# Band attention and a bilinear unit on one core: global queries over six spans of three key chunks instead of eight spans of two, with a new order of all steps

## The chip, the cores and the metric

One core of a Trainium2 chip runs the whole kernel. The metric is the device time of one execution in microseconds; the time before is the median of three runs.

## What is computed

For 8 batches and 8 heads of 64 columns there are 512 local tokens, each of which attends to the local tokens at most 32 away and to 32 global tokens, and the 32 global tokens, which attend to all 544 keys. The result goes through a bilinear unit and two products.

```python
s_g = scale * np.matmul(q_g, k_all.transpose(0, 1, 3, 2))   # k_all: 32 global and 512 local keys
out_g = np.matmul(sm(s_g), v_all)
mask = np.abs(pos[:, None] - pos[None, :]) <= 32
s_l = np.concatenate([scale * q_l @ k_g.T, np.where(mask, scale * q_l @ k_l.T, -1e9)], axis=-1)
out_l = np.matmul(sm(s_l), v_all)
x = np.concatenate([out_g, out_l], axis=2)                  # as 8 * 544 rows of 512
out = ((x @ w1) * (x @ w2) @ w3) @ w_out
```

## The kernel before

**Units.** Attention works on pairs of heads, m = 0 to 31 (four pairs for each batch). For a pair the keys lie in an SBUF tile K with the head's 64 columns on the partitions, as 16 local chunks of 32 keys and one global chunk; a spread copy (`spread_k`, L321) puts chunk n + 1 and the global chunk side by side, so that `window(m, h, n)` (L327) reads four blocks of 32 keys at once: chunk n - 1, chunk n, chunk n + 1 and the global keys. The tile V holds the same four blocks on its four strips of 32 partitions.

**Local queries.** `scores` (L335) takes 32 products of 64x32 weights with 128 columns into one PSUM tile, VectorE takes a masked minimum of the negated scores (L356), ScalarE exponentiates (L361), VectorE transposes 32x32 blocks (L369), four DMAs write to DRAM and one reads it back with the blocks on their strips (L375, L380); `values` (L393) multiplies with V.

**Global queries.** A unit u is two pairs, that is four heads; there are 16 units. `g_scores` (L460) uses the window at the eight odd n = 1, 3, ... 15 of each pair. Only chunk n - 1 and n count there; the next chunk is masked as it comes again, and the global keys count at n = 9 alone. That is 2 pairs x 8 spans x 2 heads = 32 products. `g_minus_max` (L473) runs once for each head, `g_max` (L480) combines the minima of four partition strips in six small VectorE instructions, `g_exps` (L489) runs once for each head, the 128x1024 tile G is transposed (L369) and goes through DRAM (L375, L380), and `g_values` (L495) has eight products for each of four heads and four products of one column that sum the exponentials (L508). `g_normalize`, `g_back`, `g_copy` and `g_out` (L511 to L527) finish the unit.

**Weights and the unit after attention.** Weights arrive packed as 64-bit words and are unpacked by ScalarE and VectorE (`unpack`, L605). w3 and w_out are first multiplied with each other (`fold`, L695, 64 products of 512 columns in fp32, L698). Then `first` (L542), the gate on ScalarE and VectorE (`gate_a` to `gate_lo`, L555 to L569) and `second` (L571) run over 17 tiles of 256 tokens in four quarters each, 68 gates, with split high and low parts. A gate is: copy of one factor, multiply (L561), cast, subtraction.

**What sets the order.** Every step has a number in a table written out by hand (`ORDER_OF`, L40), and its letter picks the engine where there is a choice (A is ScalarE, D VectorE, P GpSimd). `in_order` (L190) sorts by these numbers, and each engine runs its steps in that order. All DMAs are issued from SyncE's queue. An issue in that queue waits for the DMA eight issues before it to land, besides what its buffer waits for. At the start, `warm` (L869) runs ten products of zeros on TensorE, and `constants`, `clear` and `edges` (L247 to L272) set up masks and the identity.

Of the kernel before, what the change touches and what calls it, by code (L numbers as in the profile page):

```python
# [11 lines left out]
ALU = mybir.AluOpType  # L12
# [6 lines left out]
def i(ap):  # L19
# [8 lines left out]
PAD = (48, 0)  # L28

# [11 lines left out]
    load="3 11 7 56 1 20 31 124 139 107 170 191 150 226 260 233 393 287 234 312 317 421 357 445 432 551 450 679 597  "  # L41
# [5 lines left out]
    clear="4 5 117",  # L47
    edges="12",
    warm="9",
    fetch="0 14 2 15 19 26 41 45 60 71 68 72 79 95 120 115 123 131 132 152 165 177 190 178 250 251 261 259 301 360 349  "  # L50
    "380 283 350 412 409 460 491 498 471 502 542 554 520 581 595 602 555",
    unit="16 10 17 22 21 30 28 6 35 37 29 42 33 25 50 40 32 52 58 43 59 57 51 61 65 70 85 87 89 102 86 80 98 101 92  "
# [7 lines left out]
    fold="34 64 74 94 119 138 147 160 48 93 97 109 161 166 185 208 47 67 73 113 125 127 146 149 62 66 91 122 126 137  "  # L60
    "151 159 216 218 223 231 236 242 248 253 252 254 263 290 307 309 314 316 305 318 328 330 394 425 429 436 335  "
    "363 381 382 395 402 404 410",
    w34h="A179 A217 D158 A164 A284 A322 A437 D423",
    w34l="184 219 168 171 299 329 439 431",
    vc="A23 P83 A8 A39 P298 A46 P278 P368 A516 P479 A546 A398 P559 A575 A673 D663 A801 D711 A800 D807 A881 P768  "
# [3 lines left out]
    vs="A96 P105 A84 D163 A141 A227 P194 P156 A288 P213 P271 P201 A343 A355 A240 P274",  # L69
    kc="P13 D18 A54 P53 A136 A116 P202 P200 P270 P277 P339 A336 A483 A505 A529 A530 D658 D665 P725 A695 P799 A795  "  # L70
# [3 lines left out]
    s="24 77 189 238 324 367 514 582 676 730 815 858 924 981 1058 1135 1206 1265 1334 1405 1470 1540 1621 1672  "  # L74
    "1748 1815 1892 1943 2027 2079 2164 2219",
    mm="38 44 75 55 49 36 27 63 153 103 134 104 130 155 90 135 198 196 192 210 220 197 214 195 279 246 303 280 267  "
# [10 lines left out]
    ex="99 81 76 118 88 69 78 82 167 180 176 121 203 157 129 143 239 257 206 235 241 209 258 215 297 344 345 321  "  # L87
# [11 lines left out]
    tp="181 186 207 230 264 291 353 364",  # L99
    pt="D182 A187 A228 A256 A289 D304 A383 A391",  # L100
    v="193 262 325 403 524 590 684 746 816 888 923 1038 1078 1165 1216 1276 1381 1437 1510 1547 1645 1730 1750  "
    "1839 1904 1972 2026 2121 2168 2277 2333 2355",
    iv="175 222 323 362 495 552 669 701 778 847 916 957 1048 1123 1188 1253 1292 1398 1468 1530 1604 1666 1740 1798  "
    "1868 1929 2020 2070 2150 2204 2329 2348",
    nm="199 300 346 415 549 640 693 760 840 898 944 1047 1101 1173 1244 1288 1389 1456 1527 1556 1654 1735 1791  "
    "1858 1916 1991 2049 2126 2192 2295 2337 2370",
    xt="225 310 358 424",
    xh="A232 A255 A319 D333 A369 D371 A428 A444 P686 D709 P723 A733 P796 D826 A808 D828 D970 P1012 D978 P1017 D1077  "
    "P1098 P1086 A1111 P1260 A1201 P1294 A1287 D1339 P1399 P1351 D1400 A1513 A1493 D1587 D1562 A1602 A1651 P1643  "
    "D1722 A1779 A1805 A1873 P1852 P1886 D1988 D1909 P2006 D2061 P2035 A2122 D2125 A2167 A2196 P2179 D2230 A2343  "  # L110
    "P2345 P2363 D2390 D2397 D2504 P2431 A2510",
    xl="269 266 334 340 387 414 438 585 D702 D759 P724 D734 D813 D874 D812 P873 D985 P1043 D1001 D1021 D1087 D1157  "
# [91 lines left out]
def band_attention_glu_kernel(  # L204
# [62 lines left out]
    def edges():  # L267
# [3 lines left out]
        for x in range(0, 128, 32):  # L271
            nc.gpsimd.tensor_copy(pick[x : x + 32], ident[x : x + 32, x : x + 32])  # L272
# [797 lines left out]
```

## Time and profile before

| | |
|---|---|
| median of three runs | 768.01 us (766.51 to 769.08) |
| profiled execution, its own time | 763.19 us |
| its span on the core | 761.4 us |
| mean granted TensorE clock | 0.991 |
| busy: TensorE, VectorE, ScalarE, GpSimd | 98%, 60%, 38%, 14% of the span |
| DMA queue of SyncE | 136.61 MB, 63.3% of 16 engines |

Engines are named as the profile does: PE is TensorE (PEld its weight loads), DVE VectorE, ACT ScalarE, POOL GpSimd, SP SyncE (SPq its queue of DMA issues). A PE group's "mean ns" is the length of one record, and records overlap, so busy time divided by the count is the pace. An fp32 product appears as two records. The granted clock is a share of 2.4 GHz.

### The profile page before, as it was taken

Reading aid. Unit: us, or ns where it says so; the run is one execution under the profiler, and the core shown is the slowest. Engines: PE = TensorE matmul, PEld = TensorE weight load, DVE = VectorE, ACT = ScalarE, POOL = GpSimd, SP = SyncE. Lnnn points to the kernel's source line nnn. Section 1 sums busy time; section 2 is a strip of 40 time slices with the busy share of each in tenths; the row PEclk is TensorE's granted clock in tenths of the full one; section 3 lists DMA queues with packets and bytes.
Section 4 is the critical chain, followed back from the end, with each engine's and each line's share of the span. In section 5 each row is a group of like instructions: output and inputs, shape, how many; then the busy total and the mean of one; then the engine's idle time right before and its main releaser. Section 6 shows DMA issues by size and latency. Waiting matters only on the chain.

```text
span 761.4 us, 25319 instructions
## 1 busy us (share of the span) xinstructions
PE 748.4 (98%) x10564; PEld 654.5 (86%) x10564; DVE 454.0 (60%) x1385; ACT 292.1 (38%) x904; POOL 108.0 (14%) x162
## 2 busy tenths in 40 slices
PE   5999999999999999999999999999999999999998
PEld 3455689899998999998989999999999999999997
DVE  3689787766664656565667466755566566333322
ACT  4788875544232433224515243432335311210000
POOL 2126541010301100011002011011001120100000
PEclk7999999999999999999999999999999999999999
DMA  8998987888568477565788666775675787310000
GB/s 280 305 297 261 219 244 209 237 225 234 143 179 228 125 217 197 170 167 140 205 248 221 183 169 185 203 204 148 183 226 125 202 227 209 101 58 28 1 28 28
DMA packets 97850, 138.22 MB, mean 182 GB/s; under 512 B 15656, under 2 KB 58280, under 8 KB 97736
## 3 DMA queue, kind: packets, MB, share of 16 engines
q1 hardware_dynamic: 97736, 136.61, 63.3%
q8 instruction: 83, 1.36, 0.7%
q14 instruction: 31, 0.25, 0.1%
HBM read 96.71 MB, written 39.85 MB: 179 GB/s over the span
## 4 chain that ended last, share of the span: by engine, by line
PE 95%; DVE 1%; DMA 1%; POOL 0%; SPq 0%; issue 0%; ACT 0%; DVEq 0%; POOLq 0%
PE ap L551 9%; PE acc L581 9%; PE bp L551 8%; PE bp L552 8%; PE acc L583 8%; PE bp L553 8%; PE acc L582 8%; PE ap L552 8%; PE ap L553 8%; PE w L698 8%; PE s L349 5%; PE v L399 4%; PE sg L469 2%; PE gx L505 2%; DMA q<-in_q_t_dram 1%; DMA cs<-in_cst_dram 1%
## 5 line engine op out<-in xcount | busy, mean ns | idle before, releaser
L551 PE MATMUL ap<-x,w12h 128*128 128x256 f32 x512 | 145.0, 283 | 0.0
L551 PE MATMUL bp<-x,w12h 128*128 128x256 f32 x512 | 144.1, 281 | 0.0
L552 PE MATMUL ap<-x,w12h 128*128 128x256 f32 x512 | 142.1, 278 | 0.0
L552 PE MATMUL bp<-x,w12h 128*128 128x256 f32 x512 | 142.1, 278 | 0.0
L553 PE MATMUL ap<-x,w12l 128*128 128x256 f32 x512 | 142.0, 277 | 0.0
L553 PE MATMUL bp<-x,w12l 128*128 128x256 f32 x512 | 141.9, 277 | 0.0
L361 ACT ACTIVATE P<-P,mn 128x128 f32<-128x128 f32 x256 | 100.7, 396 | 63.5 <-issue 34.3
L551 PEld LDWEIGHTS ap<-x,w12h 128*128 128x128 f32 x512 | 96.2, 188 | 3.9 <-issue 2.0
L551 PEld LDWEIGHTS bp<-x,w12h 128*128 128x128 f32 x512 | 96.2, 188 | 3.8 <-issue 1.4
L552 PEld LDWEIGHTS bp<-x,w12h 128*128 128x128 f32 x512 | 96.4, 188 | 1.9
L552 PEld LDWEIGHTS ap<-x,w12h 128*128 128x128 f32 x512 | 96.3, 188 | 1.1
L553 PEld LDWEIGHTS ap<-x,w12l 128*128 128x128 f32 x512 | 96.3, 188 | 0.0
L553 PEld LDWEIGHTS bp<-x,w12l 128*128 128x128 f32 x512 | 96.3, 188 | 0.0
L356 DVE CUSTOM_DVE_ANT_0 P<-s,cs 128x128 f32<-128x128 f32 x256 | 62.8, 281 | 34.4 <-PE s L349 31.4
L698 PE MATMUL w<-wo,w3f 128*128 128x512 f32 x128 | 61.7, 627 | 2.1 <-DVE wo L612 1.5
L315 POOL COPY V<-vg 32x1024 f32<-32x1024 f32 x29 | 30.8, 1067 | 137.3 <-PE gx L508 96.0
L698 PEld LDWEIGHTS w<-wo,w3f 128*128 128x128 f32 x128 | 24.2, 199 | 29.4 <-issue 23.1
L361 ACT ACTIVATION_READ_ACCUMULATOR P<-P,mn 128x1 f32 x256 | 48.5, 190 | 0.0
L493 ACT ACTIVATE G<-G,mg 128x256 f32<-128x256 f32 x64 | 32.0, 501 | 39.3 <-PE gx L508 19.6
L349 PE MATMUL s<-K,q 64*32 64x128 f32 x2048 | 37.8, 278 | 6.0 <-POOL K L325 5.8
L349 PEld LDWEIGHTS s<-K,q 64*32 64x32 f32 x2048 | 29.1, 107 | 14.8 <-issue 6.6
L369 DVE STREAM_TRANSPOSE P<-P 128x1024 f32<-128x1024 f32 x28 | 34.7, 1238 | 4.8 <-ACT P L361 4.8
(791 smaller groups left out, 1405.8 us busy)
## 6 DMA issues: line engine op xcount, KB each, us to landing
Pd<-P SPq DMA_DIRECT2D x112, 128.0 KB, 2.9
Pt<-Pd SPq DMA_DIRECT2D x28, 512.0 KB, 4.7
raw_w<-in_w_t_dram SPq DMA_DIRECT2D x24, 512.0 KB, 5.8
V<-in_v_t_dram SPq DMA_DIRECT2D x64, 192.0 KB, 4.5
K<-in_kp_t_dram SPq DMA_DIRECT2D x36, 272.0 KB, 3.8
V<-in_v_t_dram SPq DMA_DIRECT2D x36, 256.0 KB, 4.7
out_dram<-o SPq DMA_DIRECT2D x34, 256.0 KB, 3.2
q<-in_q_t_dram SPq DMA_DIRECT2D x32, 256.0 KB, 4.3
```

The costliest lines, as they stand in the source:

```text
L349: nc.tensor.matmul(block(st[:, h], x, 128 * g), q[64 * h : 64 * h + 64, c : c + 32], window(m, h, 4 * g + x), start=True, stop=True, skip_ ...
L356: nc.vector.tensor_tensor_reduce(T["P", m][:, :, h, g], chunks(T["s", m][:, h, 128 * g : 128 * g + 128]), chunks(masks[g]), -0.125, 3.0e38 ...
L361: nc.scalar.activation(P, P, AF.Exp, bias=T["mn", m][:, g, h : h + 1], scale=-1.0, accum_out=T["sm", m][:, g, h : h + 1])
L369: nc.vector.transpose(P, P)
L493: nc.scalar.activation(G, G, AF.Exp, bias=T["mg", u][:, n : n + 1], scale=-1.0, accum_out=T["lg", u][:, n : n + 1])
L551: nc.tensor.matmul(d, wh[:, k, c, :], x[:, 0, 0:w], start=(k == m % 2 == 0), stop=False, skip_group_check=True)
L552: nc.tensor.matmul(d, wh[:, k, c, :], x[:, 1, 0:w], start=False, stop=False, skip_group_check=True)
L553: nc.tensor.matmul(d, wl[:, k, c, :], x[:, 0, 0:w], start=False, stop=(k == 3), skip_group_check=True)
L581: nc.tensor.matmul(a, gh[:, m % 2, sl], wh, start=(m == 0), stop=False)
L582: nc.tensor.matmul(a, gh[:, m % 2, sl], wl, start=False, stop=False)
L583: nc.tensor.matmul(a, gl[:, m % 2, sl], wh, start=False, stop=(m == 7))
L698: nc.tensor.matmul(T["w34", t], T["w3f", t, j // 4][:, j % 4], T["wo"][:, j], start=(j == 0), stop=(j == 7))
```

## The change

The global scores use six windows around the chunks 1, 4, 7, 10, 13 and 15, and count three chunks in each (the last counts chunk 15 alone, and there the global keys). For each head the six windows fill two partition strips of three column groups, so that the four strips are two pairs by two halves: 24 score products and 24 value products for a unit instead of 32 and 32, two masked minima and two exponentials of 384 columns instead of four of 256, one combination of minima in place of two, a G of 768 columns instead of 1024, and 384 KB instead of 512 KB out to DRAM and back. The mask for it has one column for each block and is broadcast over 32 keys; the sum over strips picks the two strips of a pair. The constants' tile shrinks from 800 to 608 columns. Every number of the order is new; of that table one line stands here.

```diff
+MIDDLES = (1, 4, 7, 10, 13, 15)
...
-    sg="442 632 770 887 1018 1162 1304 1432 1573 1701 1845 1980 2114 2251 2326 2404",
+    sg="438 608 740 879 1013 1144 1274 1417 1530 1658 1797 1919 2045 2195 2271 2347",
...
-            nc.gpsimd.memset(mask_g[:, 0:128], 0.0)
-            nc.gpsimd.memset(mask_g[:, 128:256], -1.0e30)
-            nc.gpsimd.memset(mask_g[0:32, 192:224], 0.0)
+            nc.gpsimd.memset(mask_g[:, 0:9], 0.0)
+            nc.gpsimd.memset(mask_g[:, 9:12], -1.0e30)
+            nc.gpsimd.memset(mask_g[64:128, 2:9:6], -1.0e30)
+            nc.gpsimd.memset(mask_g[64:128, 11:12], 0.0)
+            nc.gpsimd.memset(pick, 0.0)
...
-        for m in (2 * u, 2 * u + 1):
-            for g in range(2):
-                for x in range(4):
-                    for h in range(2):
-                        to = st[32 * x : 32 * x + 32, h].rearrange("p (o a b g j) -> p o g a b j", o=2, a=2, b=2, g=2)
-                        nc.tensor.matmul(to[:, m % 2, g], T["qg", m // NP][64 * h : 64 * h + 64, m % NP],
-                                         window(m, h, 2 * (4 * g + x) + 1).rearrange("p a (b j) -> p a b j", b=2),
-                                         start=True, stop=True, skip_group_check=True)
+        for r in range(3):
+            for x in range(4):
+                m, c = 2 * u + x % 2, MIDDLES[3 * (x // 2) + r]
+                for h in range(2):
+                    to = st[32 * x : 32 * x + 32, h, 0:384].rearrange("p (a b r j) -> p r a b j", a=2, b=2, r=3)
+                    nc.tensor.matmul(to[:, r], T["qg", m // NP][64 * h : 64 * h + 64, m % NP],
+                                     window(m, h, c).rearrange("p a (b j) -> p a b j", b=2),
+                                     start=True, stop=True, skip_group_check=True)
...
+    def g_minus_max(u, h):
+        keep = mask_g.rearrange("p (s r) -> p s r", s=4).unsqueeze(3).to_broadcast([128, 4, 3, 32])
+        nc.vector.tensor_tensor_reduce(T["G", u][:, :, h],
+                                       T["sg", u][:, h, 0:384].rearrange("p (s r j) -> p s r j", s=4, r=3),
+                                       keep, -0.125, 3.0e38, ALU.add, ALU.min, T["mg", u][:, h : h + 1])
...
-        eng.tensor_copy(t[0:64], mg[64:128])
-        eng.tensor_tensor(mg[0:64], mg[0:64], t[0:64], ALU.min)
-        eng.tensor_copy(t[0:32], mg[32:64])
-        eng.tensor_tensor(mg[0:32], mg[0:32], t[0:32], ALU.min)
-        eng.tensor_copy(mg[32:64], mg[0:32])
+        eng.tensor_copy(t, mg[64:128])
+        eng.tensor_tensor(mg[0:64], mg[0:64], t, ALU.min)
         eng.tensor_copy(mg[64:128], mg[0:64])
...
-        for w in range(8):
-            g, x = divmod(w, 4)
+        for w, c in enumerate(MIDDLES):
+            y, r = divmod(w, 3)
             for n in range(4):
-                nc.tensor.matmul(o[32 * n : 32 * n + 32, 0:64], t[:, x, n, g], v(u, n, w),
-                                 start=(w == 0), stop=(w == 7), skip_group_check=True)
+                m, h = divmod(n, 2)
+                nc.tensor.matmul(o[32 * n : 32 * n + 32, 0:64], t[:, 2 * y + m, h, r],
+                                 Vs[(2 * u + m) % NV][:, c % 4, h, c // 4], start=(w == 0), stop=(w == 5),
+                                 skip_group_check=True)
```

**Where the order moves.** TensorE at the start of the program, before (`warm` are the products of zeros, `s` the first pair's scores, `w` the fold):

```order
L872 MATMUL warm<-og 128x128 x10
L349 MATMUL s_156<-K_75,q_131 32x128 x32
L698 MATMUL w_0_202<-wo,w3f_0_146 128x512
L698 MATMUL w_2_220<-wo,w3f_0_213 128x512
L698 MATMUL w_1_222<-wo,w3f_0_204 128x512
L698 MATMUL w_3_239<-wo,w3f_0_225 128x512
```

and after:

```order
L351 MATMUL s_153<-K_75,q_138 32x128 x32
L870 MATMUL warm<-og 128x128 x10
L698 MATMUL w_3_222<-wo,w3f_0_208 128x512
L698 MATMUL w_0_224<-wo,w3f_0_146 128x512
L698 MATMUL w_3_222<-wo,w3f_0_208 128x512
L698 MATMUL w_2_237<-wo,w3f_0_220 128x512 x2
```

The products of zeros, which stood first, now stand behind the first scores, and another fold comes first.

SyncE's queue at the same place, before (`raw_w` and `raw_wo` are packed weights, `cs` the constants, `K` and `q` those of the first pair):

```order
L662 DMA raw_w_0_99<-in_w_t_dram 128x1024
L308 DMA vg<-in_vg_t_dram 32x512
L662 DMA raw_w_0_102<-in_w_t_dram 128x1024
L248 DMA cs<-in_cst_dram 128x128
L250 DMA cs<-in_cst_dram 32x96 x4
L282 DMA K_75<-in_kp_t_dram 128x544
L279 DMA q_131<-in_q_t_dram 128x512
L662 DMA raw_wo_0_141<-in_wo_t_dram 128x1024
```

and after:

```order
L662 DMA raw_w_0_99<-in_w_t_dram 128x1024
L662 DMA raw_w_0_102<-in_w_t_dram 128x1024
L247 DMA cs<-in_cst_dram 128x128
L249 DMA cs<-in_cst_dram 32x96 x4
L662 DMA raw_wo_0_118<-in_wo_t_dram 128x1024
L284 DMA K_75<-in_kp_t_dram 128x544
L281 DMA q_138<-in_q_t_dram 128x512
L662 DMA raw_w_0_140<-in_w_t_dram 128x1024
```

The load of vg has left this place, the first `raw_wo` has moved ahead of K and q, and q stands eight places behind a weight load instead of behind vg.

GpSimd at the same place, before, with the copy that spreads the first K behind the constants:

```order
L268 COPY cs<-cs 128x2x96
L269 MEMSET cs 32x32
L270 MEMSET cs 32x32
L272 COPY cs<-cs 32x32 x4
L325 COPY K_75<-K_75 128x15x32
```

and ScalarE after, which now has that copy:

```order
L610 ACT_TABLE_LOAD
L610 ACTIVATE raw_w_0_99<-raw_w_0_99 128x512
L327 COPY K_75<-K_75 128x15x32
L610 ACTIVATE raw_wo_0_118<-raw_wo_0_118 128x512
L610 ACTIVATE raw_w_0_102<-raw_w_0_102 128x512
```

The copy of the first K has left GpSimd's queue, where it stood behind four steps that wait for the constants, for ScalarE's, where it stands behind one unpacking step.

## Rows read from the trace of the kernel before

**Rows 1.** The page, span and part 1: engine, busy us, share, instructions.
```profile
span 761.4 us, 25319 instructions
...
PE 748.4 (98%) x10564; PEld 654.5 (86%) x10564; DVE 454.0 (60%) x1385; ACT 292.1 (38%) x904; POOL 108.0 (14%) x162
```

**Rows 2.** Stretches: busy us (instructions) of each engine, granted clock, DMA share, GB/s.
```profile
core 0: us, PE busy (x) PEld busy (x) DVE busy (x) ACT busy (x) POOL busy (x), PEclk, DMA share, GB/s
40.00:50.00 10.00, 10.00 (x154) 5.57 (x152) 7.74 (x25) 7.77 (x21) 2.08 (x4) 1.00 1.04 329
300.00:400.00 100.00, 99.86 (x1631) 90.83 (x1630) 60.75 (x193) 35.28 (x122) 8.19 (x12) 1.00 0.66 184
```

**Rows 3.** TensorE's waits, longest and shortest of five: us in total, times, longest.
```profile
PE s L349 <- POOL K L325: 5.8, 1, 5.8
...
PE s L349 <- DMA q<-in_q_t_dram: 0.3, 1, 0.3
```

**Rows 4.** Groups by line, TensorE: busy us, mean ns, idle before.
```profile
L469 PE MATMUL sg<-K,qg 64*32 64x128 f32 x1024 | 18.5, 274 | 0.0
L505 PE MATMUL gx<-V,Gt 128*32 128x64 f32 x1024 | 17.7, 220 | 0.1
```

**Rows 5.** The chain of waits in order of time: start us, us, what.
```profile
87.70 2.58 PE w L698 x6
90.27 1.09 PE sg L469 x64
...
157.82 1.01 PE gx L505 x62
```

**Rows 6.** Groups by line, VectorE and ScalarE; last, the timeline of GpSimd.
```profile
L369 DVE STREAM_TRANSPOSE P<-P 128x1024 f32<-128x1024 f32 x28 | 34.7, 1238 | 4.8 <-ACT P L361 4.8
L475 DVE CUSTOM_DVE_ANT_0 G<-sg,cs 128x256 f32<-128x256 f32 x64 | 25.0, 412 | 17.3 <-PE sg L469 17.3
L415 DVE TENSOR_TENSOR vo<-v,si 128x512 f32<-128x512 f32 x32 | 21.9, 683 | 12.6 <-PE v L399 8.4 <-DMA vd<-vo 4.2
...
L493 ACT ACTIVATE G<-G,mg 128x256 f32<-128x256 f32 x64 | 32.0, 501 | 39.3 <-PE gx L508 19.6 <-PE ap L553 9.5 <-issue 6.8
...
8.26 0.34 POOL L268 COPY cs<-cs 128x192 f32<-128x192 f32 x1 [6.63 <-DMA cs<-in_cst_dram]
```

**Rows 7.** Timeline of TensorE, 0 to 20 us: start us, us, what, idle before.
```profile
1.00 4.47 PE L872 MATMUL warm<-og 128*128 128x128 f32 x20 [1.00 <-POOL og L254]
11.22 1.96 PE L349 MATMUL s<-K,q 64*32 64x128 f32 x64 [5.75 <-POOL K L325]
14.69 2.08 PE L698 MATMUL w<-wo,w3f 128*128 128x512 f32 x2 [1.51 <-DVE wo L612]
17.38 2.93 PE L698 MATMUL w<-wo,w3f 128*128 128x512 f32 x3 [0.61 <-DVE w3f L612]
```

**Rows 8.** Stretches around the turn of the clock, columns as in rows 2.
```profile
21.00:22.00 1.00, 1.00 (x3) 0.48 (x2) 0.00 (x0) 0.00 (x0) 0.00 (x0) 0.50 0.92 289
22.00:23.00 1.00, 1.00 (x4) 0.46 (x3) 0.76 (x2) 0.76 (x2) 0.00 (x0) 0.89 0.89 211
```

**Rows 9.** SyncE's queue: a wait, two issues; DMA issues, us to landing.
```profile
SPq L662 <- DMA raw_w<-in_w_t_dram: 1.5, 1, 1.5
...
1.65 0.42 SPq L662 DMA_DIRECT2D raw_w<-in_w_t_dram  x1
...
7.01 0.33 SPq L662 DMA_DIRECT2D raw_wo<-in_wo_t_dram  x1
...
raw_w<-in_w_t_dram SPq DMA_DIRECT2D x1, 512.0 KB, 5.3
...
raw_wo<-in_wo_t_dram SPq DMA_DIRECT2D x1, 512.0 KB, 4.2
...
q<-in_q_t_dram SPq DMA_DIRECT2D x1, 256.0 KB, 6.7
```

**Rows 10.** VectorE's waits at the gate's multiply: us in total, times, longest.
```profile
DVE bp L561 <- PE bp L553: 130.2, 53, 5.8
```

More of the change, by code (lines that the diff above doesn't have):

```diff
@@ L99 @@
[L99 to L105, printed above, removed]
@@ L175 @@
-    "2595 2603",
-    second="508 515 563 588 615 627 657 659 713 721 763 771 794 797 824 830 866 875 909 913 940 953 975 980 1020 1024  "
[6 rows of a table removed]
-    out="A691 A699 D852 A855 D1014 D1016 A1144 D1153 A1262 D1266 A1395 A1401 D1551 A1558 A1688 A1697 D1829 D1836  "
-    "D1967 D1971 D2109 D2116 A2228 A2233 A2346 A2364 A2460 A2462 A2526 A2528 D2569 A2571 D2609 A2610",
-    store="729 914 952 1040 1121 1061 1232 1388 1322 1505 1544 1606 1569 1614 1716 1877 1937 1907 2065 2208 2141 2306  "
-    "2256 2442 2349 2424 2505 2490 2539 2538 2590 2591 2611 2612",
+    load="3 14 7 67 47 20 30 118 116 103 175 209 162 242 333 264 350 266 275 388 282 427 428 473 456 437 502 686 581  "
[5 rows of a table added]
@@ new lines @@
+    clear="5 4 9",
+    edges="10",
+    warm="25",
+    fetch="0 6 15 16 2 28 34 45 57 35 60 64 102 89 104 113 115 161 185 164 191 192 198 247 207 251 276 283 312 286 353  "
+    "374 183 267 352 402 481 488 499 478 509 542 549 526 587 593 600 580",
+    unit="8 1 19 17 13 27 23 22 26 29 38 41 18 21 32 33 39 40 44 48 55 70 73 86 71 66 79 53 50 68 90 81 101 98 83 105  "
[7 rows of a table added]
+    fold="43 62 78 87 117 132 149 157 63 77 84 96 112 171 184 196 54 61 74 93 114 138 142 148 42 49 94 95 139 140 145  "
+    "147 213 218 223 224 229 238 262 263 237 245 271 272 274 277 287 288 294 313 319 334 358 359 364 372 369 371  "
@@ new lines @@
+    "D2317 P2325 D2370 D2443 D2369 D2434",
+    tn="461 503 622 680 747 801 876 916 1000 1058 1165 1194 1267 1336 1429 1477 1539 1596 1690 1714 1811 1865 1931  "
+    "1992 2062 2120 2224 2264",
+    po="493 540 625 689 758 804 901 966 1003 1075 1166 1199 1291 1359 1443 1483 1544 1614 1703 1764 1836 1886 1949  "
+    "2001 2084 2133 2226 2265",
+    pi="511 578 645 714 793 839 923 995 1022 1093 1189 1234 1326 1392 1451 1512 1565 1630 1727 1803 1851 1920 1963  "
+    "2046 2091 2188 2242 2278",
@@ new lines @@
+    gd="844 936 1047 1147 1329 1418 1609 1762 1869 2036 2132 2270 2339 2350 2398 2411",
+    gin="2414 2430 2436 2437",
+    gxh="P2416 A2431 D2441 A2447",
+    gxl="P2424 P2435 P2442 D2448",
+    first="449 458 440 464 485 504 505 508 533 543 548 561 606 652 616 654 660 666 675 684 701 705 709 718 722 750 756  "
[12 rows of a table added]
+    ga="A471 A512 A584 A655 A690 A708 D759 D790 D819 D862 D892 A913 D969 D993 A1017 D1071 A1108 A1123 D1139 D1169  "
[3 rows of a table added]
+    gb_="475 528 585 657 692 720 763 809 835 872 902 933 973 1024 1042 1079 1122 1142 1181 1200 1241 1285 1312 1341  "
@@ new lines @@
+    "2100 2134 2161 2183 2227 2254 2273 2310 2334 2363 2384 2400 2419 2433 2454 2466 2476 2486 2496 2509 2518  "
+    "2528 2540",
+    second="514 525 560 590 626 627 671 677 723 732 755 765 805 808 825 836 869 871 885 899 926 929 955 970 991 1007  "
[6 rows of a table added]
+    out="A695 A713 A838 D868 A984 A985 A1133 D1135 A1215 D1242 A1370 D1395 A1508 D1509 A1647 D1656 D1755 A1760 A1929  "
+    "D1942 A2069 D2071 A2169 D2198 A2286 A2289 A2397 D2404 A2458 D2462 D2504 A2507 A2543 A2546",
+    store="842 751 887 1021 1037 1154 1237 1233 1293 1364 1427 1597 1540 1664 1675 1897 1884 1786 2011 2056 2090 2233  "
@@ L187 @@
+    "2211 2296 2309 2376 2429 2415 2489 2533 2532 2531 2547 2548",
 )
@@ L233, in band_attention_glu_kernel @@
     ps_1 = ctx.enter_context(tc.tile_pool(name="ps_1", bufs=1, space=PSUM))
-    cs = const.tile([128, 800], F32, tag="cs", name="cs")
-    ident, pick = cs[:, 0:128], cs[:, 768:800]
-    mask = cs[:, 128:768].rearrange("p (n c) -> p n c", n=5)
+    cs = const.tile([128, 608], F32, tag="cs", name="cs")
+    ident, pick = cs[:, 0:128], cs[:, 528:592]
+    mask = cs[:, 128:512].rearrange("p (n c) -> p n c", n=3)
     masks = [mask[:, x] for x in (0, 1, 1, 2)]
-    mask_g = cs[:, 512:768]
+    mask_g = cs[:, 512:524]
     og = const.tile([128, 128], F32, tag="og", name="og")
@@ L372, in turned_out @@
         P = flat(T[kind, m])
-        d = T[kind + "d", m] = dram.tile([128, 4, 256], F32, tag=kind + "d", name=f"{kind}d{m}", bufs=3)
+        c = P.shape[1] // 4
+        d = T[kind + "d", m] = dram.tile([128, 4, c], F32, tag=kind + "d", name=f"{kind}d{m}", bufs=3)
         for x in range(4):
@@ L379, in turned_in @@
         t = T[kind + "t", m] = p2.tile([128, 1024], F32, tag=kind + "t", name=f"{kind}t{m}", bufs=2 if kind == "P" else 1)
-        nc.sync.dma_start(t, T.pop((kind + "d", m)).rearrange("p x c -> p (x c)"))
+        d = T.pop((kind + "d", m)).rearrange("p x c -> p (x c)")
+        nc.sync.dma_start(t[:, 0 : d.shape[1]], d)
     def transposes(m, h):
@@ L489, in g_exps @@
-    def g_exps(u, n):
-        if n == 0:
-            T["lg", u] = p2.tile([128, 4], F32, tag="lg", name=f"lg{u}", bufs=1)
-        G = T["G", u][:, :, n].rearrange("p s g j -> p s (g j)")
-        nc.scalar.activation(G, G, AF.Exp, bias=T["mg", u][:, n : n + 1], scale=-1.0, accum_out=T["lg", u][:, n : n + 1])
+        G = p2.tile([128, 1024], F32, tag="G", name=f"G{u}", bufs=NG)[:, 0:768]
+        T["G", u] = G.rearrange("p (s h r j) -> p s h r j", s=4, h=2, r=3)
+        T["mg", u] = p2.tile([128, 2], F32, tag="mg", name=f"mg{u}")
@@ L495, in g_values, with g_exps @@
+    def g_exps(u, h):
+        if h == 0:
+            T["lg", u] = p2.tile([128, 2], F32, tag="lg", name=f"lg{u}", bufs=1)
+        G = T["G", u][:, :, h].rearrange("p s r j -> p s (r j)")
+        nc.scalar.activation(G, G, AF.Exp, bias=T["mg", u][:, h : h + 1], scale=-1.0, accum_out=T["lg", u][:, h : h + 1])
     def g_values(u):
-        t = T.pop(("Gt", u)).rearrange("p (x n g q) -> p x n g q", x=4, n=4, g=2)
+        t = T.pop(("Gt", u))[:, 0:768].rearrange("p (x h r q) -> p x h r q", x=4, h=2, r=3)
@@ L507, in g_values @@
         for n in range(4):
-            nc.tensor.matmul(o[32 * n : 32 * n + 32, 64:65], pick, T["lg", u][:, n : n + 1], start=True, stop=True,
-                             skip_group_check=True)
+            m, h = divmod(n, 2)
+            nc.tensor.matmul(o[32 * n : 32 * n + 32, 64:65], pick[:, 32 * m : 32 * m + 32], T["lg", u][:, h : h + 1],
+                             start=True, stop=True, skip_group_check=True)
     def g_normalize(u):
@@ L835, in global_pair @@
         read(("sg", u), ("qg", b), ("K", m - 1), ("K", m))
-        for x in range(1, -1, -1):
-            for h in range(2):
-                add(("gm", m - x, h), "DVE", [("sg", u), ("edges",)], g_minus_max, m - x, h)
-                read(("gm", m - x, h), ("sg", u))
-        gm = [("gm", m - x, h) for x in range(2) for h in range(2)]
+        for h in range(2):
+            add(("gq", u, h), "DVE", [("sg", u), ("edges",)], g_minus_max, u, h)
+            read(("gq", u, h), ("sg", u))
         take("mt", 1, ("mt", u), ("gr", u))
-        add(("gr", u), "DVE", gm, g_max, u, nc.vector)
+        add(("gr", u), "DVE", [("gq", u, 0), ("gq", u, 1)], g_max, u, nc.vector)
         take("lg", 1, ("lg", u), ("ge", u, 0))
-        for n in range(4):
-            add(("ge", u, n), "ACT", [("gr", u), *[("ge", u, 0)] * (n > 0)], g_exps, u, n)
-            read(("ge", u, n), ("mg", u))
-        add(("gt", u), "DVE", [("ge", u, n) for n in range(4)], turn, "G", u)
+        for h in range(2):
+            add(("ge", u, h), "ACT", [("gr", u), *[("ge", u, 0)] * h], g_exps, u, h)
+            read(("ge", u, h), ("mg", u))
+        add(("gt", u), "DVE", [("ge", u, n) for n in range(2)], turn, "G", u)
         take("Gd", 3, ("Gd", u), ("go", u))
```

134 lines of the change are left out of this document (53 added, 81 removed), and 126 rows, old and new, of tables (ex, first, ga, gh).

## The prediction

> **What bounds the kernel now.** I read the page's first lines first: TensorE is busy 748.4 of 761.4 us, VectorE 454.0 [rows 1], so at most 13.0 us of the span could come from better feeding of TensorE, and the rest only from giving it less to do. Then the stretches: between 40 and 50 us its busy time is the whole stretch, between 300 and 400 us 99.86 of 100 us, while VectorE has some 40% to spare in the second [rows 2]. Then TensorE's waits: there are five in the whole run, the longest (5.8 us) for the first K window, the shortest 0.3 us for a q load [rows 3]; none is for a global step. So the path is TensorE's own queue from about 17 us to the last matmul, and anything taken out of that queue is worth its full time as long as its feeders stay early. That is the argument of this prediction.
>
> **Removed from TensorE.** Four heads' global scores take 32 matmuls now (eight spans, two pairs, two heads), 24 after; their value products 32 now, 24 after; the four sum-picking matmuls stay. An fp32 matmul of either kind shows as two records: 1024 records are 16 units of 64 [rows 4]. A scores group of 64 records lasts 1.09 us on the chain of waits, 17.0 ns per record; 62 records of a value group last 1.01 us, 16.3 ns per record [rows 5]. A new group has the same tile shapes in the same rotation over the array (four column strips, two row halves for scores; four column strips for values), so I price a removed record at the pace of the group: 16 units x 16 records x 17.0 ns = 4.35 us for scores and 16 x 16 x 16.3 ns = 4.17 us for values, together **8.5 us**. Bounds: if one record's own duration (274 ns and 220 ns [rows 4]) is a fixed part of each group, the pace is (1.09 - 0.27) / 63 = 13 ns, and 512 records give 6.7 us; by total busy time, 18.5 and 17.7 us for 1024 each [rows 4], a quarter is 9.1 us. I take 8.5, since the chain is where the time is really passed on.
>
> For the removed tiles the trace says 16 to 17 ns each. The Trainium skill ("TensorE: Matmul & The Clock Gate", Part 3, Measured speedup vs the span model) has packed tiles cost only about 4 ns each beyond the first; by that the 512 records would be worth an estimated 2 us. The trace does not agree. A rival below carries that case in the kernel's own terms.
>
> **Removed beside TensorE.** VectorE's masked minimum goes from 64 instructions of 412 ns on 256 columns to 32 on 384; even at 1.5 x 412 ns that is 19.8 us instead of 26.4. The cross-partition maximum goes from six small instructions to three per unit, the transposition covers 768 instead of 1024 columns, ScalarE's global exponentials go from 64 of 501 ns to 32 of at most 752 ns [rows 6], and each unit's trip through DRAM from 512 KB to 384 KB out and in. All of that lies under TensorE, which waits for none of it [rows 3]; I cost it at nothing. Its worth is cover: feeders get earlier. What no row shows is the masked minimum with a mask broadcast over 32 columns and one more dimension. The nearest row is the normalising multiply, which also broadcasts an operand: 683 ns for 512 columns [rows 6], no slower per column than the present minimum. Even at double price (32 x 0.8 us) VectorE would be no busier than now, so both ends are zero on the path. The changed memsets stand in GpSimd's queue ahead of the 6.63 us that it waits for the constants [rows 6].
>
> **Moved: the start.** Everything has a new place, but only before 22 us did TensorE wait for more than 0.3 us, so only there do I price the order. Now: the warming matmuls run from 1.00 for 4.47 us, then TensorE is idle until the first scores at 11.22 (1.96 us), does one fold matmul at 14.69, and from 17.38 [rows 7] runs on with no other wait than the 0.3 us [rows 3]. The granted clock is still 0.50 (the 1.2 GHz level) between 21 and 22 us and turns to 2.4 GHz early in the next microsecond [rows 8], about 22.2. So 4.8 us of folding ran at half speed and lost 2.4 us. A fold record takes 0.43 us at the full clock (2.58 us for six [rows 5]), a fold matmul 0.86. Counted as a stream at full clock that began with the first fold, it began at 17.38 + 2.4 - 0.86 = 18.9 us.
>
> After: first scores, then the warming matmuls, then folds. The first scores no longer stand behind GpSimd's constants (the K copy is on ScalarE), but their q load is one place later than a weight load, and it is the tenth DMA. Now the eleventh, the first wo load, waited 1.5 us for a raw weight load to land (the third DMA, issued at 1.65 and 5.3 us under way) and was issued at 7.01; it landed 4.2 us later, at 11.2, with twice the bytes of q [rows 9]. A DMA thus waits for the one eight places earlier. For the tenth that was vg, and is a weight load after the change, so q takes over that wait; issued near 7 and at wo's delay it lands near 11 us, at the delay of the second q load (6.7 us [rows 9]) near 13.7. I take 11.2, the time of today's first scores. Scores and warming then last 1.96 + 4.47 = 6.4 us, to 17.6, with no break on TensorE. If the clock is up by then, the stream begins at 17.6 and 1.3 us is gained; if it rises during the warming, which then gets shorter, about 2 us; if it stays low for the first folds as long as today, 2.4 us are lost again and the start is 1.1 us worse; a late q adds 2.5 us to that. Today the clock rose in unbroken work after a start with breaks; after the change the unbroken work begins some 6 us earlier, so I lean to the first case and take **1.0 us gained**, between 2 gained and 2 lost, with 3.6 lost as the far corner. The first fold's weights would have to pass VectorE by 17.6; today its counterpart came at 17.38, so this is close and is one reason why I don't take more.
>
> **Sum.** 8.5 + 1.0 = 9.5 us. The profiled execution took 763.19 us, so 753.7. That execution lies below all three runs shown (766.51 to 769.08), so I carry the ratio over: 768.01 x 753.7 / 763.19 = 758.5 us. About 0.3% (2.3 us) can be told from no change.
>
> **Rivals.**
> - *Weight supply in the fold stage.* Between 40 and 50 us the DMA engines are at a share of 1.04 with 329 GB/s [rows 2]; a 512 KB weight load is 1.6 us of that. In the new order two loads more ahead of one that a fold waits for would cost TensorE 3.2 us. Today not one fold after 17.38 waited. Together with a start that loses 1 us: 8.5 - 3.2 - 1.0 = 4.3 us, 763.7 us. Chance 0.12.
> - *The removed tiles overlapped.* If a group's length is mostly filling and switching, its 16 missing records save little: at a quarter of the shown pace 512 x 4 ns = 2 us, with the start 3.0 us, so 765.0 us. Against it: value groups of 62 and score groups of 64 records both fit one price per record, although their records last 220 and 274 ns [rows 4, 5]. Chance 0.04. The span model of the Trainium skill named above would give this.
> - *The gate becomes the wait (slower).* A second product waits for multiply, cast and subtraction of its gate, in VectorE's queue. If the new order leaves a P transposition of 1.24 us [rows 6] ahead of the multiply, TensorE stands for up to that long. There are 68 gates; the 9.5 us gained and the 2.3 us that can be told are used up from ten fully exposed gates on, and with 15 of them the time is 758.5 + 15 x 1.24 = 777 us. Against it: VectorE was early at 53 of those multiplies and waited 130.2 us there, 2.5 us on average [rows 10], and it now has less to do. Chance 0.05.
> - *The work does not leave.* The order of TensorE holds 24 and 24 matmuls per unit, so this rival has no room.
>
> **How the numbers follow.** Forecast 0.77, supply rival 0.12, overlap 0.04, gate 0.05; 0.02 for a start better than I allow. The bounds of removed work (6.7 to 9.1) and start (-2 to 2) give 4.7 to 11.1 us gained, 757 to 763.3 us; the runs shown differ by 1.3 us from their median, so the range is 755.5 to 764.0, which also takes in the supply rival. Faster by over 0.3%: forecast, supply, the better start and about half of the overlap case make 0.93; I take 0.05 off for the supply and the late start in full together: 0.88. Within 0.3%: 0.06. Slower: 0.06.
>
> **What would show it.** Right: 768 score and 768 value records with groups near 0.82 and 0.8 us; TensorE's busy time down by about 8 us; at most some tenths of waiting after 20 us; the clock at 2.4 GHz before 20 us. Wrong: a wait of TensorE behind a fold or an acc product that is not among today's five; groups that stay at 1 us with fewer records; first scores later than 13 us.

## The result, and the profile after

The changed kernel takes a median of 757.24 us (756.74 to 757.95, 4 runs) against 767.26 us (766.11 to 769.08, 4 runs) for the kernel before on the same chip: a ratio of 0.9868, 95% interval 0.9845 to 0.9891. That is 1.3% faster, 1.3 us below the predicted 758.5 us and inside the range. The profiled execution took 757.95 us, the slowest of its four, while the profiled one of before, 763.19 us, lies below all the four runs beside it; the two profiled times therefore differ by 5.2 us only, and the medians by 10.0.

The page's first lines of the changed kernel:

```profile
span 756.1 us, 24124 instructions
...
PE 738.3 (98%) x10052; PEld 647.6 (86%) x10052; DVE 424.8 (56%) x1249; ACT 287.8 (38%) x861; POOL 112.1 (15%) x167
```

Against [rows 1], TensorE's busy time fell by 10.1 us and the span by 5.3 us. The time without work therefore grew, from 13.0 to 17.8 us. Both halves need an explanation. First the busy time, in the groups by line of the changed kernel (busy us, mean ns, idle before):

```profile
L698 PE MATMUL w<-wo,w3f 128*128 128x512 f32 x128 | 59.2, 599 | 3.1 <-issue 2.5 <-DVE wo L612 0.7
...
L474 PE MATMUL sg<-K,qg 64*32 64x128 f32 x768 | 15.0, 275 | 0.0
L503 PE MATMUL gx<-V,Gt 128*32 128x64 f32 x768 | 13.9, 220 | 0.0
```

and the fold's line of the kernel before in the same view:

```profile
L698 PE MATMUL w<-wo,w3f 128*128 128x512 f32 x128 | 61.7, 627 | 2.1 <-DVE wo L612 1.5 <-DVE w3f L612 0.6
```

The global scores lost 18.5 - 15.0 = 3.5 us and the value products 17.7 - 13.9 = 3.8 us [rows 4], together 7.3 us. The same 128 fold records cost 2.5 us less, since the folds no longer begin at half pace. That is 9.8 of the 10.1 us. A mean of 275 ns against 274 says nothing about the gain: the records overlap, and only busy time and the length of a group carry it. The chain of waits of the changed kernel (start us, us, what) has the groups:

```profile
91.87 0.87 PE sg L474 x48
...
114.25 1.09 PE s L351 x64
...
127.31 0.79 PE gx L503 x46
```

The score group went from 1.09 to 0.87 us and the value group from 1.01 to 0.79 [rows 5], each for 16 records less: 0.22 / 16 = 13.75 ns per record, not 17.0 and 16.3. Some 0.2 us of a group does not shrink with its records. The local scores, whose 64 records nobody touched, still take 1.09 us.

Now the idle time: all of TensorE's waits in the changed kernel (us in total, times, longest), and its timeline up to 22 us:

```profile
PE s L351 <- ACT raw_w L610: 10.2, 1, 10.2
PE w L698 <- issue: 2.5, 1, 2.5
PE v L403 <- DMA Pt<-Pd: 0.7, 2, 0.4
PE w L698 <- DVE wo L612: 0.7, 1, 0.7
```

```profile
10.16 1.96 PE L351 MATMUL s<-K,q 64*32 64x128 f32 x64 [10.16 <-ACT raw_w L610]
12.05 4.55 PE L870 MATMUL warm<-og 128*128 128x128 f32 x20
16.44 5.74 PE L698 MATMUL w<-wo,w3f 128*128 128x512 f32 x13
```

The start is as the change has it: first scores, products of zeros, folds, without a break. The thirteen fold records run at 5.74 / 13 = 0.44 us each, which is the full pace of 0.43 us [rows 5], so the folds' stream begins at 16.44 us where it began at 18.9 by the prediction's count: 2.5 us gained. The wait of 10.16 us ahead of it, which the profile lays to an unpacking, ended with the first q: its load was issued at 6.04 us and landed at 10.03, 0.13 us before the first scores. After 20 us, however, TensorE waits 2.5 + 0.7 + 0.7 = 3.9 us where before it waited for 0.3 us [rows 3], and the longest of these waits has no releaser. Counted in records done, the changed kernel leads the kernel before by 2.6 us at 26 us, by 1.2 us at 35 us, after the wait for wo, and is 1.6 us late at 52 us, after the longest wait. The start gave, and something later took back more. The experiments ask what each half of the change is worth, and what this wait is.

VectorE and ScalarE went as costed. Their groups of the changed kernel:

```profile
L480 DVE CUSTOM_DVE_ANT_1 G<-sg,cs 128x384 f32<-128x384 f32 x32 | 17.1, 544 | 10.5 <-PE sg L474 10.4
```

```profile
L494 ACT ACTIVATE G<-G,mg 128x384 f32<-128x384 f32 x32 | 19.5, 610 | 24.4 <-DVE mg L488 8.6 <-PE gx L508 8.0 <-issue 6.0
```

The masked minimum with the broadcast mask takes 544 ns for 384 columns against 412 ns for 256 [rows 6], that is 1.32 times; I had allowed for 1.5 times, and double as the far end.

### The profile page after: what moved, and what is told of

Its sections match the earlier page's. It is cut to its first block, busy times and chain, and to the rows that moved or that the text cites. A ratio compares the mean times of both kernels' runs of the same rounds, so it can differ in the third digit from the quotient of the medians.

```text
span 756.1 us, 24124 instructions
## 1 busy us (share of the span) xinstructions
PE 738.3 (98%) x10052; PEld 647.6 (86%) x10052; DVE 424.8 (56%) x1249; ACT 287.8 (38%) x861; POOL 112.1 (15%) x167
## 4 chain that ended last, share of the span: by engine, by line
PE 92%; DMA 4%; issue 1%; SPq 1%; ACT 0%; POOL 0%; DVE 0%; POOLq 0%; ACTq 0%
PE bp L551 8%; PE ap L551 8%; PE acc L581 8%; PE acc L583 8%; PE bp L552 8%; PE bp L553 8%; PE acc L582 8%; PE ap L552 8%; PE ap L553 8%; PE w L698 6%; PE s L351 4%; PE v L403 4%; DMA Pt<-Pd 2%; PE sg L474 2%; PE gx L503 1%
## 5 line engine op out<-in xcount | busy, mean ns | idle before, releaser
L698 PE MATMUL w<-wo,w3f 128*128 128x512 f32 x128 | 59.2, 599 | 3.1 <-issue 2.5
L351 PE MATMUL s<-K,q 64*32 64x128 f32 x2048 | 37.8, 278 | 10.2 <-ACT raw_w L610 10.2
L327 POOL COPY K<-K 128x480 f32<-128x480 f32 x27 | 17.0, 638 | 171.4 <-DMA K<-in_kp_t_dram 161.4
L317 POOL COPY V<-vg 32x1024 f32<-32x1024 f32 x25 | 26.4, 1064 | 71.0 <-PE gx L508 57.0
L403 PEld LDWEIGHTS v<-V,Pt 128*32 128x32 f32 x2048 | 30.2, 110 | 7.9 <-issue 5.8
```

The source lines that it names most:

```text
L317: (nc.scalar.copy if eng is nc.scalar else eng.tensor_copy)(to, src)
L351: nc.tensor.matmul(block(st[:, h], x, 128 * g), q[64 * h : 64 * h + 64, c : c + 32], window(m, h, 4 * g + x), start=True, stop=True, skip_ ...
L403: nc.tensor.matmul(vt[32 * x : 32 * x + 32, g, h], t[:, x, h, g], Vs[m % NV][:, x, h, g], start=True, stop=True, skip_group_check=True)
L698: nc.tensor.matmul(T["w34", t], T["w3f", t, j // 4][:, j % 4], T["wo"][:, j], start=(j == 0), stop=(j == 7))
```

## The experiments

The first question was how much is the shorter groups and how much the new order. Four kernels ran on one chip, beside the kernel before at 765.96 us. In the tables below every number is of one of the two kernels, so one line shows the edit.

**Six spans in the old order (six_old).** The code of the changed kernel with the table of before:

```diff
-    sg="438 608 740 879 1013 1144 1274 1417 1530 1658 1797 1919 2045 2195 2271 2347",
+    sg="442 632 770 887 1018 1162 1304 1432 1573 1701 1845 1980 2114 2251 2326 2404",
```

> The changed kernel's code (six spans) in the order of the kernel before: each step keeps its old number, the two new minima and exponentials of a unit take two of the four old places. Theory (removed products are worth their time on TensorE wherever they stand, the order is worth only the start): about 7.3 to 8.5 us below the kernel before, ratio 0.989 to 0.9905, TensorE's waits as before (first scores near 11.2, first stream of folds near 17.4). Rival (the new order carries the gain, the shorter groups only open waits elsewhere): within 3 us of the kernel before, with new waits of TensorE.

Measured: 757.55 us (756.01 to 759.25, 6 runs), ratio 0.9887, interval 0.9857 to 0.9918. This is the changed kernel's time within what can be told. The profile shows two opposite halves that cancel:

```profile
PE s L259 <- POOL K L235: 4.8, 1, 4.8
PE w L606 <- DVE wo L520: 2.1, 1, 2.1
PE w L606 <- DVE w3f L520: 1.8, 1, 1.8
PE warm L778 <- POOL og L161: 1.0, 1, 1.0
PE gx L411 <- DMA Gt<-Gd: 0.3, 1, 0.3
```

All of these waits but the last lie before 20 us, as in the kernel before; none is laid to issue, the profile's word for a wait without a releaser. TensorE is busy 742.2 us, 3.9 more than in the changed kernel, of which the folds make 62.2 - 59.2 = 3.0; it is idle for 13.9 us instead of 17.8. Both spans are 756.1 us.

**Eight spans in the new order (eight_new).** The code of before with the new table (each number of a global exponential or minimum taken twice):

```diff
-    sg="442 632 770 887 1018 1162 1304 1432 1573 1701 1845 1980 2114 2251 2326 2404",
+    sg="4380 6080 7400 8790 10130 11440 12740 14170 15300 16580 17970 19190 20450 21950 22710 23470",
```

> The code of the kernel before (eight spans) in the order of the changed kernel; the four minima and four exponentials of a unit stand in the two places of the new ones. Theory: only the start gains, 1 to 2.4 us below the kernel before (ratio 0.997 to 0.9987), first scores near 10.2 and folds from 16.4. Rival (the order carries the gain): 5 us or more below. Rival (the new order only fits with the lighter VectorE): slower than the kernel before, with TensorE waiting behind the minimum or the gate.

Measured: 778.12 us (775.29 to 778.83), ratio 1.0147, interval 1.0112 to 1.0182: 12 us slower than before, from an order that costs nothing with six spans. The first scores start at 9.64 us, so the start is there; but 9.7 us of TensorE's waits are laid to nothing the profile shows ("issue"), 1.1 us to a gate, and a piece of the chain shows what such a stop looks like:

```profile
515.56 1.09 PE sg L375 x64
516.65 1.02 PE v L305 x60
517.66 2.25 issue
519.92 0.41 PE v L305 x3
520.33 1.64 PE gx L411 x60
```

Three groups of small products stand behind each other, and TensorE stops inside the second, four records before its end. This stop costs twice. The stretches after it in the same kernel (PE busy, PEld, DVE, ACT and POOL busy, granted clock, DMA share, GB/s):

```profile
518.00:520.00 2.00, 0.08 (x2) 0.08 (x4) 1.45 (x6) 0.00 (x0) 0.00 (x0) 0.98 0.50 78
520.00:521.00 1.00, 1.00 (x41) 1.00 (x45) 0.59 (x1) 0.00 (x0) 0.00 (x0) 0.50 0.83 308
...
524.00:525.00 1.00, 1.00 (x11) 1.00 (x10) 0.60 (x2) 0.00 (x0) 0.00 (x0) 1.00 0.02 8
```

After the stop the granted clock is 0.50, the 1.2 GHz level, and the value group takes 1.64 us instead of 1.01. This part is booked as busy time, not as waiting.

**The two kernels once more (before_again, after_again).** No edit; they ran to see whether the changed kernel's wait without a releaser, and the calm of the kernel before, are properties of the kernels or of one execution.

> The kernel before, unchanged, for a second profile. Its first profiled execution took 763.19 us and its runs 766.1 to 769.1. If the profiled one was a lucky execution (a stall that most executions have was missing), this profile is near 767 and shows a wait of TensorE of some us, likely one that the profile lays to issue, that the first did not have. If profiling makes it faster by itself, it is near 763 again with the same five waits.

> The changed kernel, unchanged, for a second profile. If the 2.45 us before a fold record at 49.6 us (laid to issue) belongs to the order, it stands there again; if it is an accident of one execution, it is gone or elsewhere and the profiled time is up to 2.5 us lower than 757.95. Time of the runs near 757.

Measured: 766.19 us (764.5 to 768.84, 12 runs), ratio 1.0001, and 757.99 us (756.26 to 761.8), ratio 0.9899, interval 0.9866 to 0.9933. The kernel before has no wait laid to issue in this profile either, and TensorE is busy 748.4 us as in the first. The changed kernel has two again, at 50.30 us and, new, inside a value group at 501.80 us:

```profile
PE v L403 <- issue: 1.6, 1, 1.6
...
PE w L698 <- issue: 1.2, 1, 1.2
```

So, of these four kernels, the stops come with the two in the new order. In the changed one, the stop near 50 us stands before the same record in both profiles, after 347 records; the other stop is in one of them only.

My theory then was that long unbroken runs of small products outrun the supply of instructions. Three kernels were made for it, and one for the start; they ran on one chip beside the kernel before at 767.47 us.

**Small groups moved apart (after_spread, eight_new_spread).** In each order 30 of the local and global score and value steps (s, v, sg, vg) were moved by one to three larger steps, which breaks up 22 of the 25 places where such groups touch. One line of it, where all other numbers are the old ones times 100:

```diff
-    sg="438 608 740 879 ...
+    sg="43800 61601 74000 87900 ...
```

> The changed kernel with the same 30 moves. Theory: its stops laid to issue (2.5 and 2.8 us in its two profiles) go, 754 to 756 us, 2 us below the changed kernel. Rival (the moves delay what waits for the groups): equal or slower, with new waits behind the normalisation or a P tile.

> The eight-span kernel in the new order (12 us slower than the kernel before), with 30 of TensorE's small groups (scores and value products) moved by a few steps so that 22 of the 25 places where two or three such groups stand directly behind each other are broken up by the unit's products. Theory (TensorE runs dry of instructions in such places: it stops inside a group, while one 16 KB instruction packet lands): most of the 9.7 us that its trace lays to issue goes, 765 to 770 us, at most two such stops left. Rival (these stops are hidden waits for data of the new order): the stops stay and the time stays within 3 us of 778, or gets worse, since the products come later.

Measured: 769.28 us (766.63 to 772.62, 12 runs), ratio 1.0024, interval 1.0009 to 1.0039; and 788.36 us (783.22 to 791.02), ratio 1.0270, interval 1.0238 to 1.0301. The gain that the theory asked for did not come: by the medians, from two chips, both are 10 to 12 us slower than the kernels that they were made from. The stops did not all go: in the first 3.0 us stay (against 2.5 and 2.8 in the two profiles of the unspread kernel), in the second they fall from 9.7 to 4.1. What I had left out is the price of the break. TensorE is busy 746.6 us in the first for exactly the changed kernel's products, which took 738.3 and 736.3 us. Its chain shows why:

```profile
307.49 0.12 PE ap L461
307.61 1.09 PE s L259 x64
308.70 0.32 PE ap L459
309.01 0.12 PE ap L460
...
311.65 0.87 PE sg L382 x48
312.52 0.43 PE acc L489
312.95 0.23 PE acc L490
```

The first large product behind a group of small ones takes 0.32 us instead of 0.12, and 0.43 instead of 0.23: 0.20 us for each small run between large products. Counted over the timelines by the tiles, TensorE changes from 128x128 to smaller tiles and back 62 times in the changed kernel, 65 times in the order of before, and 92 times here: 30 more than in the changed kernel, or 6.0 us. The remaining 2.3 to 4.3 us of busy time have no place that I found. New waits for gates and copies make some 3 us more. The Trainium skill ("TensorEngine Tiling (Array Packing)", Tiling Modes, Key Properties) says that a change of the tiling mode drains TensorE, without a price; the trace agrees, with 0.20 us for a change and back.

**Three times the score products (before_triple).** The kernel before issues its global score products three times into the same place:

```diff
-        for m in (2 * u, 2 * u + 1):
+        for m in (2 * u, 2 * u + 1) * 3:
```

> The kernel before with each unit's 32 global score products issued three times over (same places, same values), which makes every group 192 records long. Price per record: 13.75 ns from the two group lengths (1.09 us for 64, 0.87 for 48) gives 28 us more, the mean of 17 ns gives 35. Theory (instructions run dry in long runs of small products): beside that, stops laid to issue inside these groups, 0.5 to 2 us in many of the 16, so 800 us or more. Rival (no such limit): no stops, 794 to 801.

Measured: 816.52 us (814.0 and 819.04), ratio 1.0639, interval 1.0599 to 1.0680. TensorE is busy 781.3 us, 32.9 more for 2048 records more: 16.1 ns each. This is not the price of a record, as the groups with a stop are drawn longer besides (1.66 + 1.54 us for the two parts of one). A tripled group without a stop lasts 2.83 us, the first line below, where it lasted 1.09: 13.6 ns for each of its 128 more records. And 18.0 us are laid to issue, of which the score groups have 11.0 in eight stops; one of them stands in the lines behind it:

```profile
126.61 2.83 PE sg L469 x192
...
285.36 2.41 PE sg L469 x161
287.76 1.89 issue
289.66 0.67 PE sg L469 x31
```

The products behind this stop are repetitions of ones that were done just ahead of it, on the same operands and into the same tile. No operand can have been late. The stop belongs to the run of products, not to a feeder. What supports instructions as the cause is the count of packets on the instruction queue in the pages (the kernel before; the changed kernel; this one):

```profile
q8 instruction: 83, 1.36, 0.7%
```

```profile
q8 instruction: 79, 1.29, 0.7%
```

```profile
q8 instruction: 99, 1.62, 0.8%
```

That is 16 packets more for 2048 records and 4 fewer for 512: one packet for 128 records, 256 instructions with their weight loads. In a long run of small products such a packet is used up in 128 x 17 ns = 2.2 us or less, among the gate's products, at 0.12 us each, in some 15 us. The Trainium skill ("Runtime: NRT & Kernel Launch", Instruction fetch mechanics) has instructions arrive in blocks of 16 KiB, or 256 instructions, and crossing into the next one mostly hidden. The packets agree with the block; "mostly hidden" holds among large products here, not where a block is nearly all small products. Whether TensorE waits for such a block is taken up behind the last runs.

**Only the products of zeros moved (six_old_warm).** The old order with one number changed:

```diff
-    warm="9",
+    warm="245",
```

(the others times ten).

> Six spans in the old order, with the products of zeros alone moved behind the first scores, as the new order has it. Theory (the start gains since the clock is up before the folds): no idle TensorE between first scores and warming, folds from 16.8 to 17.5 at the full clock, 2 us below the same kernel without the move (757.6), so 755.5. Rival (the folds wait for their weights anyway): the second fold still begins at 18.4 and little is gained, 757.

Measured: 757.53 us (756.75 to 759.58), ratio 0.9878, interval 0.9858 to 0.9898: no difference from six_old. The folds begin at full pace at 17.32 us, but the first K is still copied by GpSimd, and the first scores come at 11.57 us instead of 10.44. Small stops of 0.8, 0.7 and 0.5 us stand later in the profile. Whatever the start alone is worth, it is less than this comparison can tell.

The last two kernels put back the removed products and nothing else. They ran together, beside the kernel before at 766.64 us.

**The removed products put back (six_old_refill, after_refill).** In either order a unit has 32 and 32 products again, by repeating some:

```diff
-        for r in range(3):
+        for r in (0, 1, 2, 2):
...
-        for w, c in enumerate(MIDDLES):
+        for w, c in [(0, MIDDLES[0])] * 2 + list(enumerate(MIDDLES)):
```

> The six-span code in the old order with the removed products put back: the last third of the score products is issued twice and the first four value products of a head group three times, so a unit has 32 and 32 products again (1024 records of each), while VectorE, ScalarE and the transfers keep their smaller work. Theory, the products alone carry the gain of six_old: 512 records more at 13.75 to 17 ns are 7 to 8.5 us over the 757.5 us of six_old, 764.5 to 766 us, a ratio to the kernel before of 0.995 to 1.0. Rival, the lighter work beside TensorE carries a good part of it: 760 us or less, a ratio below 0.993.

> The changed kernel in its own order with the same products put back, so groups of 64 records stand in the new order with the light work beside TensorE. Theory, long runs of small products are what cost eight_new its 12 us: stops laid to issue come back, 8 to 10 us of them, and the time is 773 to 779 us, a ratio to the kernel before of 1.008 to 1.016. Rival, in eight_new the heavier work of the other engines (masked minima, exponentials, transfers of eight spans) came late in an order made for less of it: then only the products' own 7 to 8.5 us return, 765 to 767 us, a ratio of 0.997 to 1.0.

Measured, old order: 766.59 us (765.02 to 768.84, 12 runs), ratio 0.9999, interval 0.9986 to 1.0012. With the products back, the whole gain is gone, although VectorE is still busy 435.8 us instead of 454.0 and the transfers stay smaller. The work beside TensorE was worth nothing, as costed. Between six_old and this kernel TensorE's busy time grew from 742.2 to 750.0 and the span from 756.1 to 764.0, 7.8 and 7.9 us, 15 ns per record; the medians, from two chips, differ by 9.0.

Measured, new order: 770.74 us (768.96 to 773.82), ratio 1.0056, interval 1.0034 to 1.0079. This lies between the two expectations, 13.5 us above the changed kernel. Stops laid to issue come back, 6.5 us of them:

```profile
PE gx L503 <- issue: 2.7, 2, 1.5
PE w L698 <- issue: 2.4, 1, 2.4
PE v L403 <- issue: 1.4, 1, 1.4
```

One of them on the chain, again inside a run:

```profile
478.00 1.03 PE v L403 x64
479.03 0.88 PE gx L503 x61
479.91 1.54 issue
481.46 0.20 PE gx L503
```

TensorE is busy 6.8 us more than in the changed kernel, the stops are 4.0 us more, and the waits for unpacked weights 1.4 us more. So longer groups in this order bring stops back, which is a part of eight_new's loss. The eight-span code with its heavier work beside TensorE is 7.4 us slower still (778.12 against 770.74, on two chips), of which the profiles show 3.2 us in further stops, 1.1 us for a gate and stretches at the half clock like the one above. That the heavier work brings the further stops is not shown.

**Where the stops stand.** If a stop is a wait for the next block of 256 instructions, only whole blocks can lie between two stops. This profile, cut in the middle of its four stops (stretch, its length, TensorE's busy us and records, granted clock, DMA share, GB/s):

```profile
0.00:51.00 51.00, 38.05 (x347) 1.00 0.89 291
51.00:156.70 105.70, 103.48 (x1652) 1.00 0.83 238
156.70:319.70 163.00, 161.68 (x2543) 1.00 0.65 181
319.70:480.70 161.00, 159.65 (x2544) 1.00 0.65 177
```

1652 records are 13 times 127.1, and 2543 and 2544 are 20 times 127.2: with their weight loads and the waits for semaphores among them, 127 records are a block. The first stop comes after 347 records in all nine profiles that have one near 50 us. Over the twelve profiles 40 stops are laid to issue. Counted in all instructions of TensorE's queue, 38 of them come after 193 and a whole number of times 256, and each of these 38 ends 2.3 to 3.1 us after a packet of the instruction queue began to move; two, of 0.8 and 0.3 us in six_old_warm and after_spread, do neither. So these stops are waits for the next block, whatever the products in it. They come where a block is used up quickly: of 34 blocks that lasted under 2.6 us, 26 ended in a stop, of 36 between 2.6 and 4 us 7, and of 910 longer ones 5. This is read from the traces; no run changed the blocks alone. The kernel before has one block under 2.6 us and the changed kernel one, eight_new has six, before_triple fifteen.

## Why the prediction was right, and where it was not

- **Bound: right.** TensorE's queue sets the time: put the products back and the time of before returns (ratio 0.9999).
- **Removed from TensorE, 8.5 us: right in kind, somewhat large by the rows.** The groups' shrinkage gives 512 x 13.75 ns = 7.0 us, the groups' busy time 7.3, the busy time with the products put back 7.8, the medians 8 to 9. The forecast groups of 0.82 us came at 0.87. The step that failed is the price per record: I divided the whole group by its records, and so gave every record its share of about 0.2 us that stays with the group. The value that I used as a lower bound, 13 ns with a fixed part, was the better description; the range held it. Groups tripled in length bear it out: 13.6 ns for a record more, where no stop falls into them.
- **The rival of overlapped tiles (4 ns each): did not happen**; a record is worth 13.6 ns at least.
- **Removed beside TensorE, nothing: right**, shown by six_old_refill.
- **Start, +1.0 us: right in sign, too small.** 2.5 us were gained in the profile: the first scores came at 10.16, not 11.2, and the folds had the full pace from the first on. The q load was what the first scores waited for, as I had it, but it was issued at 6.04 us, not near 7, and landed at 10.03; and the first folds' weights were there in time.
- **Everything later, nothing: wrong, and hidden by the start.** "At most some tenths of waiting after 20 us" became 3.9 us. The weight-supply rival named 3.2 us for the same stage, but only the 0.7 us for wo is of its kind; the 2.5 us has no feeder at all: it stands at the end of an instruction block. I had not thought of a stop without a releaser, since before showed none. It stood before a fold, so one of the named signs of being wrong came true, with the total inside the range all the same. The new order as a whole is therefore worth nothing that six spans can show: six_old at 0.9887 and the changed kernel at 0.9868 and 0.9899 overlap.
- **The gate's rival: did not happen.** VectorE was early at 50 of the gate's multiplies and waited 136.0 us there (130.2 at 53 before [rows 10]), and TensorE waited for no gate, in its second profile for 0.3 us; in eight_new it did, for 1.1 us.
- **The total: right by the medians (10.0 us against 9.5), less so by the rows, and in part by luck.** The profiled execution was forecast at 753.7 us and took 757.95. In its rows TensorE is busy 10.1 us less (7.3 for the products, 2.5 for the folds), waits 1.3 us longer before the folds (10.2 against 1.0 + 5.75 + 1.51 + 0.61 = 8.9 [rows 7]) and 3.6 us longer behind them: 5.2 us gained, as the spans have it (5.3). The second pair of profiles has 763.1 and 754.5 us, 8.6 apart. Single executions of either kernel differ by up to 7 us within one set of runs, and both profiled ones of before lie below their medians. What the medians have more than the rows is not explained by any of these runs: by the rows a price too high, a start too small and a loss left out make 5.2 us of the 9.5, and that the medians come so near to the forecast is to this extent luck.

No kernel run here beats the changed one by more than the intervals; six_old and six_old_warm equal it. What stays open: why one block of under 2.6 us ends in a stop and another does not, in the kernel before and in different executions of one kernel, and what the medians have beyond the rows.

## What to carry over

Price removed small products by the difference between two lengths of a group, not by a group's length over its count: the fixed 0.2 us at the edges stays. On an engine that is 98% busy, the count of changes between small and large products and the number of instruction blocks that are nearly all small products, and so quickly used up, are both costs of an order, and they pull against each other: quick blocks ended in stops here, and groups set apart paid at their edges. Where a wait has no releaser, count the instructions up to it. Before believing in an order, run it with the code of before, and the code with the order of before; here the second took the whole gain.

## What the runs showed of the hardware

- TensorE stops for 0.2 to 2.7 us at the end of a block of 256 instructions, without a releaser in the profile, mostly where the block lasted under 2.6 us, and goes on 2.3 to 3.1 us after an instruction packet began to move. Waits laid to issue make 18.0 us in before_triple, 9.7 in eight_new, 6.5 in after_refill, 0.8 in six_old_refill, none in the kernel before.
- After a stop of 2.25 us in eight_new the granted clock fell to 0.50 and was back at 1.00 four us later, so the time lost is larger than the wait that the profile names. After stops of 1.5 us in after_refill it stayed at 1.00, and so it did after the 2.45 us stop of the changed kernel, where the next folds ran at 0.43 us a record.
- A run of small tiles between large products costs TensorE 0.20 us in the first large product behind it, after 48, 64 and 192 records alike.
- The granted clock's rows do not tell the pace at the start: they have 1.00 in the first microseconds of the changed kernel, while the twenty records of the products of zeros take 4.55 us; in its second profile they take 3.58 us. In six_old they have 1.00 from 18 to 23 us, while five fold records from 18.41 us on take 4.63 us, about half the full pace.
